# Two indirect transfers of an expert loop put behind relus by one-element VectorE copies

## The chip, the cores and the metric

The kernel runs on one core of a Trainium2 chip. The metric is the device time of one execution in microseconds, the median over several runs. Before the change it is 409.39 us (3 runs, 408.94 to 409.46).

## The reference

Attention with normalised queries and keys over 8 batches of 12 heads, 448 positions of width 64. Its output, read as 3584 tokens of width 768, goes through a mixture of 8 experts, each of which keeps at most 80 tokens:

```python
logits = x @ w_gate                       # x: attention output, 3584 x 768
expert_idx = np.argmax(logits, axis=1)    # gate_w: softmax share of that expert
out = np.zeros((N, D))
for e in range(E):                        # 8 experts
    tok_idx = np.where(expert_idx == e)[0]
    # over 80 tokens: keep the 80 with the largest gate_w
    h = np.maximum(x[tok_idx] @ w1[e], 0.0)
    out[tok_idx] = gate_w[tok_idx, None] * (h @ w2[e])
```

## The kernel before

Most of the time is the attention, which writes its unnormalised output rows (768 values and 12 row factors, so 780 floats) to the DRAM scratch `xr_dram`. The change lies wholly behind it, in the expert loop at the end. The text counts experts from 0 to 7, as the code does: the fourth is expert 3, the seventh is expert 6.

For each expert, `gather(e)` (L1107) issues an indirect DMA from the POOL queue that fetches 80 rows of 780 floats (250 KB) into a tile `xg`; `normal(e)` (L1153) multiplies them by their row factors in three VectorE instructions of 256 columns each (tile `xn`, L1157); `xpose(e)` (L1162) turns `xn` in six TensorE transposes (tile `pxt`, L1172) and copies the result to `xgT`. The loop (L1181) then does, for expert `e`, 48 matmuls with `w1` into `ph` (L1188) in two halves, each ended by a relu on ScalarE into `h_sb` (L1192); then `normal` and `xpose` of expert `e+1`; then the issue of `gather(e+4)`, which is held by a one-column memset of its tile (`wait=True`, L1118); then 16 matmuls with `w2` into two `py` (L1219); then two VectorE multiplications by the gate weights into `yo` (`weighted`, L1224); and `scatter` (L1203), an indirect DMA from the POOL queue that writes the 80 rows of `yo` to the output. Expert 0 differs: expert 1 is turned between its matmuls with `w2`, and `normal(2)` follows them. The last expert has four `py` of 192 columns and scatters in two halves.

Gathers 1, 2 and 3 are issued before the loop. POOL issues its transfers in the order of the program: gathers 1, 2, 3 and 4, scatter 0, gather 5, scatter 1, gather 6, and so on, each waiting at the head of POOL's queue until its own semaphores are there. They all travel in the DMA queue q0.

SP issues the weight loads, in queue q1, in program order: a part of expert 5's `w2` (`fetch_part`, L924; its last two of eight rows of blocks are held by a memset, L927, that stands inside `normal(1)`, behind its first multiplication), and, as each of experts 0 and 1 sets its weight buffers free, `w1` and `w2` of experts 6 and 7 (`fetch_late`, L242), 1536 KB each. The order of all this is the order of the program text: no scheduler moves it.

Of the kernel before, what the change touches and what calls it, by code (L numbers as in the profile page):

```python
# [15 lines left out]
U32 = mybir.dt.uint32  # L16
# [5 lines left out]
def kernel(  # L22
# [13 lines left out]
    nc = tc.nc  # L36

    B, H, S, D = q.shape
    N, DM = out.shape
    E = moe_w_gate.shape[1]  # L40
    F = moe_w1.shape[2]
    CAP = int(moe_capacity)
# [16 lines left out]
    FC = F // 128  # L59
# [139 lines left out]
    def load_weights(pool, e, slot, early=None):  # L199

        w1 = []
        for n, (c0, c1) in enumerate(((0, DC), ) if early is None else ((0, NE), (NE, DC))):
            if n == 0 and early is not None:
                w1.append(early)
                continue
            w1.append(pool.tile([128, c1 - c0, F], BF16, tag=f"w1_{slot}", name="w1_sb"))
        w2_sb = pool.tile([128, FC, DM], BF16, tag=f"w2_{slot}", name="w2_sb")
        w_tiles[e] = (w1, [w2_sb])

    def chunk(e, i, c):  # L210
        ts = w_tiles[e][i]
        return ts[0][:, c] if len(ts) == 1 or c < NE else ts[1][:, c - NE]
# [9 lines left out]
    def staged(e, i):  # L222
        return wb_dram[e - NW0, i].rearrange("(c p f) -> p c f", p=128, c=(DC, FC)[i])

    mark = cpool.tile([1, 4 * (E - NW0) + 2], BF16, name="mark")
# [12 lines left out]
    def fetch_late(e, parts=(0, 1)):  # L238
        for i in parts:
            ts = w_tiles[e][i]  # L240
            if len(ts) == 1:
                nc.sync.dma_start(out=ts[0][:], in_=staged(e, i))  # L242
            else:
                nc.sync.dma_start(out=ts[1][:], in_=staged(e, i)[:, NE:])
# [21 lines left out]
    with av_stack:  # L266
# [548 lines left out]
        for g in range(NG):  # L815
# [18 lines left out]
            if g < NG - 2:  # L834
                i = g % NQ
# [46 lines left out]
        for e in range(E):  # L882
            for i in range(2):
                n = 2 * e + i
# [35 lines left out]
    mpool = mlate[0]  # L920

    FE = FC - 2

    def fetch_part(c, held=False):  # L924
        t = w_tiles[NW0 + 2][1][0]
        if held:
            nc.vector.memset(t[:, c.start, 0:2], 0.0)  # L927
        nc.sync.dma_start(out=t[:, c], in_=staged(NW0 + 2, 1)[:, c])
# [80 lines left out]
    def rows_normal(i, xn, xg):  # L1009
        c = slice(256 * i, 256 * i + 256)  # L1010
        return (xn[:, c].rearrange("p (hh u d) -> p u hh d", hh=2, u=2),
                xg[:, c].rearrange("p (u hh d) -> p u hh d", hh=2, u=2),
                xg[:, DM + 4 * i:DM + 4 * i + 4].rearrange("p (u hh) -> p u hh", hh=2)
                .unsqueeze(3).to_broadcast([CAP, 2, 2, D]))

    for h in range(4):
        u, hh = divmod(h, 2)
        o = hh * 128 + u * D
# [85 lines left out]
            chosen(1, False)  # L1104
    outs = dram_disjoint_views(out, E + 1)
    xgs = {}
    def gather(e, wait=False):  # L1107

        if e == 1:
            xgs[e] = tpool.tile([128, 1024], F32, tag="beat", name="xg")[:CAP, :XW]  # L1110
        elif e % 4 == 3:
            xgs[e] = prep.tile([128, NJ + 1, 256], F32, tag="xb", name="xg")[
                :CAP].rearrange("p j d -> p (j d)")[:, :XW]
        else:
            xgs[e] = upool.tile([128, 2, S], F32, tag="us", name="xg")[:CAP].rearrange(
                "p u s -> p (u s)")[:, :XW]
        if wait:
            nc.vector.memset(xgs[e][:, 0:1], 0.0)  # L1118
        nc.gpsimd.indirect_dma_start(
            out=xgs[e], out_offset=None, in_=xr_dram[:, :],  # L1120
            in_offset=bass.IndirectOffsetOnAxis(ap=idxG[:, e:e + 1], axis=0))

    gather(1)
    idxT = tpool.tile([CAP, E], U32, name="idxT")
    nc.vector.tensor_copy(idxT[:, :], psc[:CAP, 1, :E])
# [27 lines left out]
    def normal(e, behind=None):  # L1153
        xg = xgs[e]
        xn = mpool.tile([CAP, DM], BF16, tag="xn", name="xn")
        for i in range(NQ):
            nc.vector.tensor_mul(*rows_normal(i, xn, xg))  # L1157
            if behind and not i:
                behind()
        return xn  # L1160

    def xpose(e, xn):  # L1162
        xgT = mpool.tile([128, DC, CAP], BF16, tag="xgT", name="xgT")
        pxt = mps.tile([128, DC, CAP], BF16, tag="pxt", name="pxt", bufs=1)
        if e > 1:
            o = [pxt[:, c] for c in range(DC)]
        else:
            first = tpps.tile([128, 2, 1024], BF16, tag="tp", name="pxt")[:, 0, :DC // 2 * CAP]
            o = [first[:, c * CAP:c * CAP + CAP] for c in range(DC // 2)]
            o += [pxt[:, c] for c in range(DC // 2)]  # L1170
        for c in range(DC):
            nc.tensor.transpose(o[c], xn[:, c * 128:(c + 1) * 128], identb[:CAP, :CAP])  # L1172
        if e > 1:
            nc.vector.tensor_copy(xgT[:], pxt[:])
        else:
            by_two(xgT, [first, pxt[:, :DC // 2].rearrange("p c t -> p (c t)")])
        xts[e] = xgT

    for e in range(2, 4):
        gather(e)  # L1180
    for e in range(E):  # L1181
        h_sb = mpool.tile([128, FC, CAP], BF16, tag="hsb", name="h_sb")
        for fh in range(2):
            ph = mps.tile([128, FC // 2, CAP], F32, tag="ph", name="ph")
            for f4 in range(FC // 2):
                fc = fh * (FC // 2) + f4
                for c in range(DC):
                    nc.tensor.matmul(ph[:, f4, :],  # L1188
                                     chunk(e, 0, c)[:, fc * 128:(fc + 1) * 128],
                                     xts[e][:, c, :],  # L1190
                                     start=(c == 0), stop=(c == DC - 1))
            nc.scalar.activation(h_sb[:, fh * (FC // 2):(fh + 1) * (FC // 2), :],  # L1192
                                 ph[:], AF.Relu)
        if e + 1 < E and e != 1:
            xn = normal(e + 1, (lambda: fetch_part(slice(FE, FC), True)) if not e else None)
        if 0 < e < E - 1:
            xpose(e + 1, xn)
        if e < E - 4:
            gather(e + 4, wait=True)
        DN = DM // 2  # L1200
        yo = mpool.tile([CAP, DM], F32, tag="yo", name="yo", bufs=3)

        def scatter(half=None):  # L1203
            if half is None:
                o, at, y, n = outs[e], idxT[:, e:e + 1], yo[:, :], N
            else:
                o = outs[e + half].rearrange("n (h d) -> (n h) d", h=2)
                at, y, n = idxL[:, half:half + 1], yo[:, half * DN:half * DN + DN], 2 * N
            nc.gpsimd.indirect_dma_start(  # L1209
                out=o[:, :], out_offset=bass.IndirectOffsetOnAxis(ap=at, axis=0),  # L1210
                in_=y, in_offset=None, bounds_check=n - 1, oob_is_err=False)

        pw = DN if e + 1 < E else DN // 2
        pys = [mps.tile([CAP, pw], F32, tag=("py", "py", "pz", "pxt")[i], name="py",
                        bufs=2 if i < 2 else 1) for i in range(DM // pw)]

        def product(i, fcs):
            for fc in fcs:
                nc.tensor.matmul(pys[i][:, :], h_sb[:, fc, :],  # L1219
                                 chunk(e, 1, fc)[:, i * pw:i * pw + pw],  # L1220
                                 start=(fc == 0), stop=(fc == FC - 1))

        def weighted(i):
            nc.vector.tensor_scalar(yo[:, i * pw:i * pw + pw], pys[i][:, :], gwT[:, e:e + 1],  # L1224
                                    None, op0=ALU.mult)

        if e + 1 < E:
            for fh in range(2):
                for i in range(2):
                    if not e and fh and i:  # L1230
                        xpose(1, xn)
                    product(i, range(fh * (FC // 2), (fh + 1) * (FC // 2)))
            if not e:
                xn = normal(2)
            for i in range(2):
                weighted(i)
            scatter()
        else:
            for fh in range(2):
                for i in range(2):  # L1240
                    product(i, range(fh * (FC // 2), (fh + 1) * (FC // 2)))
                    if fh:
                        weighted(i)
            scatter(0)
            for i in range(2, 4):
                product(i, range(FC))
                weighted(i)
            scatter(1)
        if NW0 + 3 + e < E:
            load_weights(wpool, NW0 + 3 + e, e)  # L1250
            fetch_late(NW0 + 3 + e)
# [35 lines left out]
```

## Time and profile before

| | |
|---|---|
| median of 3 runs | 409.39 us |
| the profiled execution, device time | 408.7 us |
| its span, first to last instruction | 407.0 us |
| its TensorE clock, mean granted | 0.999 of full speed |
| TensorE (PE) busy | 395.7 us, 97% |
| VectorE (DVE) busy | 352.2 us, 87% |
| ScalarE (ACT) busy | 320.6 us, 79% |
| GpSimd (POOL) busy | 90.2 us, 22% |
| bytes moved by DMA packets | 100.92 MB |

The profile is of one execution, and its times count from the span's first instruction. 1.7 us of the device time lie outside the span. A row of the timeline gives the start, the time until the last instruction of the group ended, the engine, the line and operation, the tiles written and read, how many instructions were merged, and in brackets how long the engine had been idle and what ended that. A DMA instruction's own duration is its issue; its transfer's time, from issue to landing, stands in the DMA view, where median and value are the same if one transfer was issued in the stretch.

### The profile page before, as it was taken

The page shows a single profiled execution, that of the slowest core. Times are in us where ns is not written, and L with a number is a line of the kernel's source. Part 1 is how long each engine was busy: PE and PEld are TensorE (multiplying, and loading weights), DVE is VectorE, ACT ScalarE, POOL GpSimd, SP SyncE. Part 2 cuts the span into 40 slices and gives each one's busy share as a digit, 9 for nine tenths or more (in the row PEclk, how much of TensorE's full clock was granted, in tenths as well). Part 3 has the DMA queues.
Part 4 walks back from the last instruction along what each step waited for, and adds up shares of the span by engine and source line. Part 5 has one row for each costly group of instructions (what it writes and reads, how often), then busy time and mean ns, then how long its engine had stood idle before and what let it go on. Part 6 is the DMA issues. An engine that isn't in the chain of part 4 may idle for free.

```text
span 407.0 us, 12628 instructions
## 1 busy us (share of the span) xinstructions
PE 395.7 (97%) x5285; PEld 195.4 (48%) x5285; DVE 352.2 (87%) x658; ACT 320.6 (79%) x508; POOL 90.2 (22%) x150
## 2 busy tenths in 40 slices
PE   8999999999999999999999999999999999999994
PEld 7334444444444444444444444444443453458884
DVE  5899987998999999997999999979999968876552
ACT  6899979997989889988899799979897877572110
POOL 7200002501031012220251024020512020154322
PEclk9999999999999999999999999999999999999999
DMA  7459999999989999989999999999999759798991
GB/s 244 144 159 212 272 296 257 273 217 304 254 223 264 246 260 263 294 205 228 243 306 217 243 278 230 289 237 285 219 205 297 161 195 374 245 277 274 342 333 52
DMA packets 76105, 100.92 MB, mean 248 GB/s; under 512 B 8448, under 2 KB 65280, under 8 KB 76048
## 3 DMA queue, kind: packets, MB, share of 16 engines
q1 hardware_dynamic: 60176, 70.99, 54.7%
q0 software_dynamic: 15872, 29.13, 39.3%
q8 instruction: 41, 0.67, 0.6%
q14 instruction: 16, 0.13, 0.1%
HBM read 101.11 MB, written 39.89 MB: 346 GB/s over the span
## 4 chain that ended last, share of the span: by engine, by line
PE 73%; DVE 12%; ACT 8%; issue 5%; POOL 2%; POOLq 0%; DVEq 0%
PE ps L423 26%; PE po L440 25%; PE zl L475 5%; DVE sm L458 4%; PE tp L381 4%; PE xp L381 3%; DVE ms L314 2%; DVE qn L344 2%; PE py L1219 2%; PE wps L894 2%; ACT at L426 1%; PE ph L1188 1%; POOL out_dram L1209 1%; ACT qkT L412 1%; PE mp L666 1%
## 5 line engine op out<-in xcount | busy, mean ns | idle before, releaser
L426 ACT ACTIVATE at<-ps 128x896 f32<-128x896 f32 x168 | 146.5, 930 | 4.5 <-PE ps L423 3.9
L423 PE MATMUL ps<-qkT 64*64 64x448 f32 x1344 | 147.3, 548 | 2.5 <-ACT row L624 1.3
L440 PE MATMUL po<-at,vt 64*64 64x448 f32 x1344 | 142.5, 537 | 0.0
L458 DVE TENSOR_TENSOR sm<-sm,at 128x896 f32<-128x896 f32 x120 | 130.7, 1089 | 3.4 <-ACT at L426 0.5
L440 PEld LDWEIGHTS po<-at,vt 64*64 64x64 f32 x1344 | 50.1, 133 | 74.0 <-issue 63.9
L423 PEld LDWEIGHTS ps<-qkT 64*64 64x64 f32 x1344 | 43.8, 132 | 66.6 <-issue 26.2
L314 DVE TENSOR_REDUCE ms<-sq 128x14 f32<-128x896 f32 (+1 forms) x50 | 52.1, 1043 | 6.9 <-ACT sq L307 6.8
L344 DVE TENSOR_TENSOR qn<-qk,rs 128x896 f32<-128x896 f32 (+1 forms) x47 | 50.5, 1077 | 1.3
L307 ACT ACTIVATE sq<-qk 128x896 f32<-128x896 f32 (+1 forms) x48 | 44.7, 930 | 2.0 <-DMA qk<-in_q_dram 1.1
L229 POOL COPY mark<-mark 1x1 bf16<-1x1 bf16 x22 | 7.8, 354 | 138.0 <-DVE mark L228 138.0
L743 ACT COPY xb<-xp 128x1024 f32<-128x1024 f32 x24 | 24.3, 1011 | 8.4 <-PE xp L381 8.3
L381 PEld LDWEIGHTS tp<-ident,qn 64*128 64x128 f32 x672 | 23.5, 139 | 12.1 <-issue 6.0
L381 PE MATMUL tp<-ident,qn 64*128 64x64 f32 x672 | 27.2, 226 | 0.3 <-DVE qn L344 0.3
L1192 ACT ACTIVATE h_sb<-ph 128x320 bf16<-128x320 f32 x16 | 7.0, 438 | 25.7 <-PE ph L1188 25.7
L447 ACT COPY us<-po 128x896 f32<-128x896 f32 (+1 forms) x24 | 21.4, 894 | 6.5 <-PE po L440 6.4
L456 DVE TENSOR_TENSOR sm<-at 128x896 f32<-128x896 f32 x24 | 26.0, 1084 | 0.1
L412 ACT COPY qkT<-tp 128x896 f32<-128x896 f32 x24 | 22.0, 917 | 3.3 <-PE tp L381 3.1
L410 ACT ACTIVATE qkT<-tp,gqk 128x896 f32<-128x896 f32 x23 | 23.6, 1025 | 0.0
L1219 PE MATMUL py<-w_sb,h_sb 128*80 128x384 bf16 (+1 forms) x144 | 22.4, 309 | 0.0
L475 PE MATMUL zl<-us,wgs 64*32 64x448 f32 x192 | 20.3, 540 | 0.0
L1224 DVE TENSOR_SCALAR yo<-py,gwT 80x384 f32<-80x384 f32 (+1 forms) x18 | 10.0, 568 | 11.7 <-PE py L1219 11.6
L475 PE MATMUL zl<-sm,zsel 64*32 64x448 f32 x192 | 20.1, 541 | 0.0
(202 smaller groups left out, 433.2 us busy)
## 6 DMA issues: line engine op xcount, KB each, us to landing
wb_scratch<-in_moe_w_dram POOLq DMA_DIRECT2D x20, 768.0 KB, 10.5
w_sb<-wb_scratch SPq DMA_DIRECT2D x8, 1536.0 KB, 11.4
vt<-in_v_dram SPq DMA_DIRECT2D x24, 448.0 KB, 7.6
out_dram<-zeros SPq DMA_DIRECT2D x28, 384.0 KB, 10.0
qk<-in_q_dram SPq DMA_DIRECT2D x23, 448.0 KB, 6.5
qk<-in_k_dram SPq DMA_DIRECT2D x23, 448.0 KB, 5.3
w_sb<-in_moe_w_dram POOLq DMA_DIRECT2D x6, 1536.0 KB, 14.9
xr_scratch<-xb SPq DMA_DIRECT2D x48, 192.0 KB, 6.7
```

Of the source, the lines that this page charges most:

```text
L307: nc.scalar.activation(o, x, AF.Square)
L314: nc.vector.reduce_sum(out=st[g]["ms"][:, a, lo:hi], in_=st[g]["sq%d" % a][:, lo:hi], axis=AX.X)
L344: e.tensor_mul(qn[:].rearrange("p (x hh) d -> p hh x d", hh=2)[:, h0:h1], qk[:, lo:hi].rearrange("p (hh x) d -> p hh x d", x=NX), rs[:, lo ...
L381: nc.tensor.transpose(o, w, one[p, p], tile_position=(p.start, 0))
L412: nc.scalar.copy(T[:], tp[:, :, :S])
L423: nc.tensor.matmul(ps[u * 64:u * 64 + 64, hh, :S], T1[d, u, x * 64:(x + 1) * 64], T0[d, u, :], start=True, stop=True)
L426: nc.scalar.activation(at[:], ps[:, :, :S], AF.Exp)
L440: nc.tensor.matmul(po[u][hh * D:(hh + 1) * D, u, :S], vt[p, hh * NX + x, :], at[p, hh, :], start=(x == 0), stop=(x == RD - 1))
L456: nc.vector.tensor_add(s["sm"][:], s["at0"][:], s["at1"][:])
L458: nc.vector.tensor_add(s["sm"][:], s["sm"][:], s["at%d" % x][:])
L475: nc.tensor.matmul(t[32 * c:32 * c + 32, r, :S], w, x, start=(i == 0), stop=(i == NQ - 1))
L1219: nc.tensor.matmul(pys[i][:, :], h_sb[:, fc, :], chunk(e, 1, fc)[:, i * pw:i * pw + pw], start=(fc == 0), stop=(fc == FC - 1))
```

## The change

`gather` gets an argument `behind`: where it is given, VectorE copies that one element into the gather's own tile first, so that the gather has to follow the copy, and the copy what wrote the element. Gather 3 leaves the place ahead of the loop and is called from inside `normal(1)`, behind its second multiplication, with an element that expert 0's second relu writes. Scatter 6 is kept back until the last expert's relus are programmed: VectorE copies one element of the last expert's second relu half to a scratch, then the 80 row numbers of expert 6 to a tile of their own, `at6`, and scatter 6 takes its rows from `at6`. Nothing else is moved.

```diff
-    def gather(e, wait=False):
+    def gather(e, behind=None, wait=False):
...
         if wait:
             nc.vector.memset(xgs[e][:, 0:1], 0.0)
+        if behind is not None:
+            nc.vector.tensor_copy(xgs[e][:1, 0:1], behind)
         nc.gpsimd.indirect_dma_start(
...
             nc.vector.tensor_mul(*rows_normal(i, xn, xg))
-            if behind and not i:
-                behind()
+            if behind:
+                behind(i)
...
-    for e in range(2, 4):
-        gather(e)
+    gather(2)
+
+    def second(i):
+        if i == 0:
+            fetch_part(slice(FE, FC), True)
+        elif i == 1:
+            gather(3, h_sb[:1, FC - 1, 0:1])
+
     for e in range(E):
...
-            xn = normal(e + 1, (lambda: fetch_part(slice(FE, FC), True)) if not e else None)
+            xn = normal(e + 1, None if e else second)
...
             for i in range(2):
                 weighted(i)
-            scatter()
+            if e + 2 < E:
+                scatter()
+            else:
+                last = scatter
         else:
+            nc.vector.tensor_copy(mark[:, :1], h_sb[:1, FC - 1, 0:1])
+            at6 = mpool.tile([CAP, 1], U32, name="at6", bufs=1)
+            nc.vector.tensor_copy(at6[:, :], idxT[:, e - 1:e])
+            last(at=at6)
             for fh in range(2):
```

How it stands on the engines, at the two places that matter. On VectorE, around `normal(1)` in expert 0's turn, before (`xn<-xg` are the multiplications, the memset of `w_sb` holds the weight part, the memset of `xg` holds gather 4; the names in brackets are semaphores, DMAHW those of transfers from SP's queue, DMASW those of POOL's):

```order
L1157 TENSOR_TENSOR xn<-xg 80x2x2x64 [waits DMASW5_49]
L927 MEMSET w_sb 128x1
L1157 TENSOR_TENSOR xn<-xg 80x2x2x64 x2
L1118 MEMSET xg 80x1
L1145 COPY xgT<-pxt 128x240 [waits DVE_49,PE_49]
```

and with the change (lines are those of the changed kernel):

```order
L1159 TENSOR_TENSOR xn<-xg 80x2x2x64 [waits DMASW5_49]
L927 MEMSET w_sb 128x1
L1159 TENSOR_TENSOR xn<-xg 80x2x2x64
L1120 CAST xg<-h_sb 1x1 [waits DMAHW5_49,DMAHW6_49,DMAHW4_49,DMAHW7_49,DMAHW2_49,Activation_49]
L1159 TENSOR_TENSOR xn<-xg 80x2x2x64
L1118 MEMSET xg 80x1
L1147 COPY xgT<-pxt 128x240 [waits DVE_49,PE_49]
```

The copy stands between the second and the third multiplication, ahead of gather 4's memset, and waits for five DMA semaphores beside ScalarE's. On VectorE in the last expert's turn, with the change (before, the two rows between the 384-column and the 192-column multiplications are not there):

```order
L1232 TENSOR_SCALAR yo<-py,gwT 80x384 [waits DMASW7_49,PE_49]
L1232 TENSOR_SCALAR yo<-py,gwT 80x384 [waits PE_49]
L1250 COPY mark<-h_sb 1x1 [waits Activation_49]
L1252 COPY at_6555<-idxT 80x1
L1232 TENSOR_SCALAR yo<-py,gwT 80x192 [waits DMASW0_49,DVE_49,PE_49]
L1232 TENSOR_SCALAR yo<-py,gwT 80x192 [waits PE_49] x3
```

The two copies stand between expert 6's last multiplication and the last expert's first. POOL's own order of transfers is the same before and after; what changes there is what gather 3 and scatter 6 wait for.

## Rows read from the trace of the kernel before

**Rows 1.** The page, busy time, share of the span, instructions of TensorE.

```profile
PE 395.7 (97%) x5285; PEld 195.4 (48%) x5285; DVE 352.2 (87%) x658; ACT 320.6 (79%) x508; POOL 90.2 (22%) x150
```

**Rows 2.** Windows of the expert loop and the end: length, busy, PEclk, DMA share, GB/s.

```profile
364.90:401.60 36.70, 36.58 (x570) 30.98 (x570) 19.61 (x51) 7.36 (x17) 12.80 (x14) 1.00 0.86 278
...
401.60:407.00 5.40, 0.00 (x0) 0.00 (x0) 0.36 (x1) 0.00 (x0) 1.14 (x2) 0.89 0.16 47
```

**Rows 3.** Timeline of TensorE: transposes of experts 1 and 3, matmuls between.

```profile
368.60 0.38 PE L1172 MATMUL pxt<-identb,xn 80*128 80x80 bf16 x6
...
374.01 1.88 PE L1188 MATMUL ph<-xgT,w_sb 128*128 128x80 bf16 x48
375.73 0.40 PE L1172 MATMUL pxt<-identb,xn 80*128 80x80 bf16 x6
```

**Rows 4.** Timeline of VectorE from 366.8 to 376.5.

```profile
366.88 0.77 DVE L1157 TENSOR_TENSOR xn<-xg 80x256 bf16<-80x256 f32 x2 [2.10 <-DMA xg<-xr_scratch,idxG]
...
367.93 0.06 DVE L1118 MEMSET xg<- 80x1 f32 x1
...
373.56 1.26 DVE L1224 TENSOR_SCALAR yo<-py,gwT 80x384 f32<-80x384 f32 x2 [1.47 <-PE py L1219]
374.75 1.08 DVE L1157 TENSOR_TENSOR xn<-xg 80x256 bf16<-80x256 f32 x3
```

**Rows 5.** Timeline of POOL from 364 to 376: gathers 3 and 4.

```profile
365.49 0.91 POOL L1119 DMA_INDIRECT xg<-xr_scratch,idxG  x1 [0.30 <-issue]
368.28 0.91 POOL L1119 DMA_INDIRECT xg<-xr_scratch,idxG  x1 [1.88 <-DVE xg L1118]
```

**Rows 6.** Timeline of ScalarE: the second relus of experts 0 and 7.

```profile
366.85 0.44 ACT L1192 ACTIVATE h_sb<-ph 128x320 bf16<-128x320 f32 x1 [0.42 <-PE ph L1188]
...
398.85 0.44 ACT L1192 ACTIVATE h_sb<-ph 128x320 bf16<-128x320 f32 x1 [0.36 <-PE ph L1188]
```

**Rows 7.** Timeline of VectorE: the memset that holds gather 7, behind DMA semaphores.

```profile
381.38 0.06 DVE L1118 MEMSET xg<- 80x1 f32 x1 [0.25 <-issue]
```

**Rows 8.** DMA issues, us to landing: gathers 3, 4 and 7, each window alone.

```profile
xg<-xr_scratch,idxG POOLq DMA_INDIRECT x1, 3.8
...
xg<-xr_scratch,idxG POOLq DMA_INDIRECT x1, 9.2
...
xg<-xr_scratch,idxG POOLq DMA_INDIRECT x1, 7.3
```

**Rows 9.** Timeline of SP's DMA queue: the held part, then three weight loads.

```profile
367.36 0.37 SPq L928 DMA_DIRECT2D w_sb<-wb_scratch  x1
367.89 0.40 SPq L242 DMA_DIRECT2D w_sb<-wb_scratch  x1
```

**Rows 10.** DMA from 369.0 to 372.6: packets; queue, packets, MB, share of 16 engines.

```profile
DMA packets 630, 1.14 MB, mean 315 GB/s; under 512 B 16, under 2 KB 254, under 8 KB 630
...
q1 hardware_dynamic: 630, 1.14, 95.6%
```

**Rows 11.** DMA from 372.6 to 377.6: the same.

```profile
DMA packets 751, 1.61 MB, mean 321 GB/s; under 512 B 35, under 2 KB 287, under 8 KB 750
...
q0 software_dynamic: 96, 0.41, 24.5%
```

**Rows 12.** Timeline of POOL from 393 to 404: scatter 6 and the last two.

```profile
398.02 0.91 POOL L1209 DMA_INDIRECT out_dram<-yo,idxT  x1 [3.71 <-DVE yo L1224]
400.92 0.91 POOL L1209 DMA_INDIRECT out_dram<-yo,idxL  x1 [1.99 <-DVE yo L1224]
402.91 0.92 POOL L1209 DMA_INDIRECT out_dram<-yo,idxL  x1 [1.08 <-DVE yo L1224]
```

**Rows 13.** Timeline of VectorE from 396 to 403: the last three groups of multiplications.

```profile
396.48 1.26 DVE L1224 TENSOR_SCALAR yo<-py,gwT 80x384 f32<-80x384 f32 x2 [1.54 <-PE py L1219]
399.90 0.74 DVE L1224 TENSOR_SCALAR yo<-py,gwT 80x192 f32<-80x192 f32 x2 [2.16 <-PE py L1219]
...
401.55 0.41 DVE L1224 TENSOR_SCALAR yo<-py,gwT 80x192 f32<-80x192 f32 x1 [0.25 <-PE py L1219]
```

More of the change, by code (lines that the diff above doesn't have):

```diff
@@ L1201, with scatter @@
         yo = mpool.tile([CAP, DM], F32, tag="yo", name="yo", bufs=3)
-        def scatter(half=None):
+        def scatter(half=None, at=None, e=e, yo=yo):
             if half is None:
-                o, at, y, n = outs[e], idxT[:, e:e + 1], yo[:, :], N
+                o, at, y, n = outs[e], idxT[:, e:e + 1] if at is None else at[:, :], yo[:, :], N
             else:
```

## The prediction

> **What bounds the kernel now.** I read the page first: TensorE is busy for 395.7 us of a span of 407.0 [rows 1]. The change touches only the expert loop, so I read the windows next. Between 364.90 and 401.60 TensorE is busy for 36.58 of 36.70 us at a granted clock of 1.00 [rows 2]: the loop has no gap in TensorE that an earlier or later transfer could give back. Behind it lie 5.40 us without a matmul [rows 2], in which the last multiplications, the last two scatters and their landing follow each other. So there are two questions: does a changed transfer become late enough to open a gap in TensorE, and does anything in the last 5.4 us move?
>
> The timelines answer where a gather is needed. Expert 3 is turned by TensorE at 375.73, directly behind 48 matmuls that began at 374.01 [rows 3]. Its rows are multiplied on VectorE from 374.75 on, as soon as the two multiplications of expert 1, begun at 373.56, are over [rows 4]; the three take 1.08 us, up to 375.83, and the transposes follow on their heels. There is no slack here: gather 3 has to land by 374.75, and each microsecond later is a microsecond of TensorE. Today it is issued at 365.49 [rows 5] and needs 3.8 us [rows 8], so it lands at 369.3, 5.4 us early.
>
> **Gather 3, step by step.** The copy stands behind the second multiplication of expert 1, which ends at 366.88 + 0.77 = 367.65 [rows 4]. The relu that it names ends at 366.85 + 0.44 = 367.29 [rows 6], before that: the wait for the relu itself costs nothing, it is the place in VectorE's order that counts. The copy also waits for five DMA semaphores, of stores long landed. The nearest row is the memset that holds gather 7, which has a like list of them ahead of it and stood 0.25 us in issue [rows 7]. That puts the copy at 367.9. Its duration no row shows: a one-column memset takes 0.06 us [rows 4], a 256-column multiplication 0.41 (half of 0.77, with the overlap); one element is nearest the memset, and I take 0.08. POOL starts a transfer 0.29 us after such a memset (367.99 to 368.28) [rows 4, 5]. Gather 3 is then issued at 367.98 + 0.29 = 368.27, 2.8 us later than today, and at the very moment at which gather 4 is issued today (368.28) [rows 5].
>
> On VectorE the insertion pushes the third multiplication to 368.0 to 368.4. TensorE turns expert 1 from 368.60 on [rows 3], so that is covered, with 0.2 us left; without that cover it would cost at most the 0.35 us of the insertion.
>
> What lies around 368.27 decides the landing. SP issues the held weight part at 367.36 and the first 1536 KB load at 367.89 [rows 9], both ahead of it. From below, the landing is gather 3's of today, 3.8 us with no weight load beside it [rows 8]: 372.1, and no loss. From above it is gather 4's, issued at this moment with the same loads ahead: 9.2 us [rows 8], landing at 377.5, a loss of 2.7 us. The nearest row is plainly gather 4's. The DMA view says why it took so long: from 369.0 to 372.6 the engines moved 630 packets, all of them of SP's queue [rows 10], although gather 4 had been issued at 368.28; only from 372.6 on does POOL's queue get a share, 24.5% [rows 11]. I take a little off the 9.2: today's gather 3, 250 KB, is still travelling until 369.3 and holds the weight loads back, and would no longer do so. At 315 GB/s [rows 10] that is up to 0.8 us; I take 0.6. So 8.6 us, landing at 376.9.
>
> Here a rule speaks for a shorter wait. The Trainium skill, "DMA: Bandwidth & Descriptors", section "Queues, rings and completion order", says that a DMA engine goes round its queues packet by packet, typically some 9 to 17 descriptors of one queue before the next. An estimate by it, at 17 descriptors of the 1.8 KB and the 20 GB/s per engine that the view gives, is a wait of 1.6 us and a landing at 373.7, in time. The trace does not agree: 630 packets of 16 engines are 39 on each without one of POOL's queue in between [rows 10], so the sum stays with the measured landing.
>
> VectorE's multiplications of expert 3 then start at 376.9 instead of 374.75, and TensorE's transposes slip by the same 2.1 us. What is queued behind the waiting VectorE instruction: the copy of `xgT`, gather 6's memset, expert 2's multiplications. They all belong to the turn that slips and are needed no earlier in it. On POOL, gather 4 follows gather 3 at 368.27 + 0.91 + 0.30 = 369.5, 1.2 us later than today, behind it in the same queue; it is needed 4.6 us (one expert) after gather 3, and one gather's bytes took less than that today [rows 8, 11]: covered. Later gathers are issued by memsets as now and have gained 2.1 us. None of the slip is made up, because TensorE is full up to the end [rows 2].
>
> **Scatter 6.** The last second relu ends at 398.85 + 0.44 = 399.29 [rows 6]. VectorE is idle there (from 397.74 to 399.90) [rows 13], so here the wait binds. Two small copies of 0.06 to 0.15 us each end at 399.5, well before the next multiplication. POOL issues at 399.8 instead of 398.02 [rows 12], and is free again 0.91 us later, at 400.7. The next scatter, 400.92 today, wants 0.30 after that: 401.0, or 401.3 if the issue takes 1.2 us. The last one comes at 402.91 [rows 12], and POOL is free for it at 402.5 at the latest. Its row holds a riddle: its input is ready at 401.55 + 0.41 = 401.96 [rows 13], and it starts 0.95 us later, where scatter 6 started 0.28 after its own (397.74 to 398.02) [rows 12, 13]. If that is tied to the scatter before it, the end moves by +0.1 to +0.4; if scatter 6's presence there caused it, by up to -0.67. I take 0.
>
> **The sum.** Against the profiled execution: 408.7 + 2.1 + 0.0 = 410.8. The median of the runs lies 0.7 above that execution, so 409.4 + 2.1 = **411.5 us**. Bounds of the main term are 0 and 2.7 us.
>
> **Rivals.** First, the gather gets its turn at once. If POOL's queue has the 24.5% of the engines from the start that it has later [rows 11], that is 79 GB/s and 3.2 us for 250 KB; added to 3.8 as a whole, landing comes between 372.1 and 375.3, and the loss is 0 to 0.5 us: 409.4 to 409.9, not slower by what can be measured. It decides at 374.75. For it speaks that gather 3 would be issued first in an empty POOL queue, where gather 4 had gather 3 ahead; against it, that gather 3's packets were gone by 369.3 and the 3.3 us after that were SP's alone.
>
> Second, that, and the last scatter loses its odd 0.67 us because scatter 6 is no longer between: 409.4 - 0.7 = 408.7, perhaps less. For it speaks only the riddle; against it, that scatter 6 comes nearer to the last two, not further away.
>
> Third, the gap in TensorE costs more than itself. Behind the last matmul the granted clock averages 0.89 over 5.4 us [rows 2], so the clock does fall when TensorE rests. If a gap of 2 us brought it to the lower of its levels (1.2 instead of 2.4 GHz) for one expert's turn, that turn of 4.6 us would double: 411.5 + 4.6 = 416. Against it, the window's mean of 0.89 says that the fall came late in those 5.4 us.
>
> That the change does nothing is no rival for gather 3: the copy is on VectorE's path whether the relu is late or not.
>
> **How the numbers follow.** Late gather, 411.5: 0.72, by itself 410.2 to 412.6 (landings of 7.4 us, near gather 7's 7.3, to 9.8, a little over the worst). In time, 409.4 to 409.9: 0.15. In time and the end shorter: 0.08. More than 412.8, by the clock or a still later landing: 0.05. The range reaches from 409.2 to 412.8 and leaves out the faster case and the slowest. A measurement of this kernel can tell about 0.2% from no change, 0.8 us, so 408.6 to 410.2 counts as the same: faster 0.06, same 0.19, slower 0.75.
>
> **What would show it.** Right: gather 3's issue near 368.3 and a landing of 8 to 9.2 us; VectorE idle before expert 3's multiplications, ended by that transfer; one gap of about 2 us in TensorE ahead of expert 3's transposes and none elsewhere; the same distances from there to the end. Wrong: gather 3 landing before 374.75, packets of POOL's queue between 369.5 and 372.6, or no gap in TensorE.

## The result and the profile after

| | before | with the change |
|---|---|---|
| median, us | 409.16 (8 runs, 408.39 to 409.76) | 412.93 (8 runs, 409.88 to 414.23) |
| ratio, 95% interval | | 1.0081 [1.0055, 1.0107] |
| profiled execution, device time, us | 408.7 | 413.63 |
| its span, us | 407.0 | 411.9 |
| its mean granted clock | 0.999 | 0.994 |

The change makes the kernel 0.8% slower, with an interval that leaves out 1. The ratio here and below is reckoned from the executions, not from the two medians, whose quotient is 1.0092 here. The executions fall into two groups: five of the eight have a mean granted clock of 0.994 and a median of 413.54 us, the other three 0.996 to 0.999 and a median of 411.34 us. This split is half of what follows.

The page of the changed kernel, TensorE's row first, answers to [rows 1]:

```profile
PE 398.6 (97%) x5285; PEld 196.7 (48%) x5285; DVE 353.0 (86%) x661; ACT 320.4 (78%) x508; POOL 90.2 (22%) x150
```

With the same 5285 matmuls TensorE is busy 2.9 us longer. Of this 0.56 us lie ahead of the expert loop (359.65 us busy against 359.09); the rest is in the loop. Something made matmuls slower there: a wait by itself adds idle time and little busy time. TensorE's waits in the expert loop, from the view of waits:

```profile
engine line waited for: us in total, times, longest us
PE pxt L1174 <- DVE xn L1159: 1.4, 1, 1.4
PE ph L1196 <- DVE xgT L1147: 0.2, 1, 0.2
```

There is one new wait, ahead of a group of transposes; the other one is there before, too. The windows of the loop, which begins at 365.97 here, with columns as in [rows 2], show both parts of the loss:

```profile
365.95:378.00 12.05, 11.10 (x188) 9.37 (x188) 5.19 (x17) 2.98 (x7) 4.92 (x6) 1.00 0.77 229
378.00:379.40 1.40, 0.80 (x8) 0.49 (x9) 1.04 (x3) 0.00 (x0) 0.00 (x0) 1.00 1.05 365
379.40:382.85 3.45, 3.45 (x13) 2.00 (x12) 0.41 (x2) 0.00 (x0) 0.91 (x1) 0.51 1.04 329
382.85:402.80 19.95, 19.95 (x313) 16.67 (x312) 11.86 (x27) 3.50 (x8) 5.15 (x5) 1.00 0.81 275
402.80:406.30 3.50, 3.50 (x58) 3.32 (x54) 1.36 (x5) 0.87 (x2) 1.30 (x2) 1.00 0.09 25
```

In the first two stretches TensorE rests for a part; in the third it is busy all the time, but PEclk is 0.51: the lower of its two levels, 1.2 GHz. Before, the same part of the loop is at 1.00 throughout [rows 2]. The timeline of TensorE says which matmuls these are, and answers to [rows 3]:

```profile
370.64 1.88 PE L1196 MATMUL ph<-xgT,w_sb 128*128 128x80 bf16 x48
372.36 0.38 PE L1174 MATMUL pxt<-identb,xn 80*128 80x80 bf16 x6
372.58 2.77 PE L1227 MATMUL py<-w_sb,h_sb 128*80 128x384 bf16 x16
375.18 1.88 PE L1196 MATMUL ph<-xgT,w_sb 128*128 128x80 bf16 x48
378.42 0.92 PE L1174 MATMUL pxt<-identb,xn 80*128 80x80 bf16 x6 [1.36 <-DVE xn L1159]
379.17 4.45 PE L1227 MATMUL py<-w_sb,h_sb 128*80 128x384 bf16 x16
383.46 1.24 PE L1196 MATMUL ph<-xgT,w_sb 128*128 128x80 bf16 x30
```

The rows at 372.58 and 379.17 are alike, 16 matmuls with `w2` each, of experts 1 and 2: 2.77 us and 4.45. The six transposes of expert 3, 0.40 us before, are strung out over 0.92, because each pair follows its own multiplication. VectorE tells what they wait for, and answers to [rows 4]:

```profile
368.70 0.77 DVE L1159 TENSOR_TENSOR xn<-xg 80x256 bf16<-80x256 f32 x2 [2.88 <-DMA xg<-xr_scratch,idxG]
369.07 0.06 DVE L927 MEMSET w_sb<- 128x1 uint32 x1
369.38 0.13 DVE L1120 CAST xg<-h_sb 1x1 f32<-1x1 bf16 x1
...
374.73 1.26 DVE L1232 TENSOR_SCALAR yo<-py,gwT 80x384 f32<-80x384 f32 x2 [1.54 <-PE py L1227]
377.94 1.09 DVE L1159 TENSOR_TENSOR xn<-xg 80x256 bf16<-80x256 f32 x3 [1.95 <-DMA xg<-xr_scratch,idxG]
```

The last row is the forecast late gather: VectorE stood 1.95 us for gather 3's rows. Its issue on POOL, and next to it SP's queue, answer to [rows 5, 9]:

```profile
369.79 0.91 POOL L1121 DMA_INDIRECT xg<-xr_scratch,idxG  x1 [3.56 <-DVE xg L1120]
371.00 0.92 POOL L1121 DMA_INDIRECT xg<-xr_scratch,idxG  x1 [0.30 <-DVE xn L1159]
```

```profile
369.17 0.37 SPq L928 DMA_DIRECT2D w_sb<-wb_scratch  x1
369.70 7.86 SPq L242 DMA_DIRECT2D w_sb<-wb_scratch  x4
```

Gather 3 goes out 0.62 us behind the held weight part and 0.09 behind the first large load. The DMA views, of its issue and of the two stretches behind it, answer to [rows 8, 10, 11]:

```profile
xg<-xr_scratch,idxG POOLq DMA_INDIRECT x1, 8.1
...
q1 hardware_dynamic: 541, 0.94, 94.1%
...
q1 hardware_dynamic: 332, 0.68, 60.3%
q0 software_dynamic: 123, 0.50, 40.6%
```

The gather takes 8.1 us to landing. From 370.1 to 373.5 (second row) every packet is of SP's queue, and so it is up to 374.0; POOL's queue shares the engines only from 374.0 to 378.0 (third and fourth row). Not all of this silence is a wait for SP. Scatter 6 of the kernel before, issued at 398.02 when SP's loads are over, has its first packet at 399.5, 1.5 us later, and in loads_later, below, where no large load is near, gather 3's first packet comes 1.7 us behind its issue (369.24 to 370.95). Here it comes 4.2 us behind it.

For the sum two more rows of before are needed, from its timeline of TensorE, which follow the last of [rows 3]:

```profile
375.96 2.77 PE L1219 MATMUL py<-w_sb,h_sb 128*80 128x384 bf16 x16
378.57 0.63 PE L1188 MATMUL ph<-xgT,w_sb 128*128 128x80 bf16 x13
```

From the start of expert 2's `ph` to that of its `py` it was 1.95 us (374.01 to 375.96) and is 3.99 (375.18 to 379.17): 2.04 more. From there to expert 3's `ph` it was 2.61 (to 378.57) and is 4.29: 1.68 more, the clock. Expert 0's turn takes 0.13 more (364.93 to 369.47 before, 365.97 to 370.64 now). That is 3.85; from the loop's first matmul to the end of the span it is 45.93 instead of 42.07, 3.86 more. The other 1.04 us by which the spans differ lie ahead of the loop, outside the change's reach; with the same first part gather_only, below, begins its loop at 365.07.

The end, on VectorE and POOL, answers to [rows 12, 13]:

```profile
404.21 0.14 DVE L1250 COPY mark<-h_sb 1x1 bf16<-1x1 bf16 x1 [1.57 <-ACT h_sb L1200]
404.28 0.13 DVE L1252 COPY at<-idxT 80x1 uint32<-80x1 uint32 x1
404.69 0.91 POOL L1217 DMA_INDIRECT out_dram<-yo,at  x1 [5.48 <-DVE at L1252]
...
405.91 0.91 POOL L1217 DMA_INDIRECT out_dram<-yo,idxL  x1 [0.30 <-DVE yo L1232]
406.44 0.41 DVE L1232 TENSOR_SCALAR yo<-py,gwT 80x192 f32<-80x192 f32 x1 [0.25 <-PE py L1227]
407.80 0.92 POOL L1217 DMA_INDIRECT out_dram<-yo,idxL  x1 [0.98 <-DVE yo L1232]
```

Scatter 6 is late, and the scatter behind it follows with 0.30 us between; the last one still starts 0.95 us after its input (406.85), as before.

### The profile page after: what moved, and what is told of

It is laid out like the page before. It is cut to its first block, busy times and chain, and to the rows that moved or that the text cites. A ratio compares the mean times of both kernels' runs of the same rounds, so it can differ in the third digit from the quotient of the medians.

```text
span 411.9 us, 12631 instructions
## 1 busy us (share of the span) xinstructions
PE 398.6 (97%) x5285; PEld 196.7 (48%) x5285; DVE 353.0 (86%) x661; ACT 320.4 (78%) x508; POOL 90.2 (22%) x150
## 5 line engine op out<-in xcount | busy, mean ns | idle before, releaser
L1227 PE MATMUL py<-w_sb,h_sb 128*80 128x384 bf16 (+1 forms) x144 | 24.1, 323 | 0.0
```

The costliest lines, as they stand in the source:

```text
L1227: nc.tensor.matmul(pys[i][:, :], h_sb[:, fc, :], chunk(e, 1, fc)[:, i * pw:i * pw + pw], start=(fc == 0), stop=(fc == FC - 1))
```

## The experiments

Kernels of one group ran on one chip beside its own runs of the kernel before: 409.07 us (31 runs) for the first group, gather_only to filled; 410.67 (27) for the second, loads_later, gather_first, later and pool_after; 409.11 (29) for the third, the last three rows. "Low clock" counts the executions with a mean granted clock of 0.995 or less; the kernel before has 6 of 87.

| kernel | median, us | ratio, 95% interval | low clock |
|---|---|---|---|
| gather_only | 412.62 | 1.0061 [1.0035, 1.0087] | 6 of 10 |
| scatter_only | 408.90 | 1.0002 [0.9975, 1.0030] | 1 of 10 |
| early_copy | 409.38 | 1.0007 [0.9986, 1.0027] | 0 of 10 |
| filled | 411.19 | 1.0054 [1.0032, 1.0076] | 0 of 10 |
| loads_later | 411.16 | 1.0018 [1.0002, 1.0034] | 0 of 10 |
| gather_first | 409.86 | 0.9985 [0.9973, 0.9997] | 0 of 10 |
| later | 413.32 | 1.0074 [1.0054, 1.0095] | 1 of 4 |
| pool_after | 410.87 | 1.0007 [0.9991, 1.0022] | 1 of 11 |
| gather_first_again | 409.24 | 0.9996 [0.9983, 1.0009] | 0 of 12 |
| held_last | 409.28 | 1.0016 [0.9993, 1.0038] | 3 of 12 |
| change_gather_first | 409.03 | 1.0000 [0.9984, 1.0017] | 1 of 12 |

**Each part alone.** gather_only has the change's first part and none of the second, scatter_only the second and none of the first. Against the change:

```diff
gather_only:
-            if e + 2 < E:
-                scatter()
-            else:
-                last = scatter
+            scatter()
         else:
-            nc.vector.tensor_copy(mark[:, :1], h_sb[:1, FC - 1, 0:1])
-            at6 = mpool.tile([CAP, 1], U32, name="at6", bufs=1)
-            nc.vector.tensor_copy(at6[:, :], idxT[:, e - 1:e])
-            last(at=at6)
scatter_only:
-    gather(2)
+    for e in range(2, 4):
+        gather(e)
...
-        elif i == 1:
-            gather(3, h_sb[:1, FC - 1, 0:1])
```

> The change without its second part: scatter 6 is issued as before, gather 3 stays behind the copy. If the loss is gather 3's lateness, this is as slow as the whole change, 1.005 to 1.011 times the kernel before, with VectorE idle for about 2 us ahead of expert 3's multiplications and gather 3 landing 8 us after its issue. If the end of the kernel (scatter 6 close to the last two scatters) makes the loss, this is within 0.2% of the kernel before.

> The change without its first part: gather 3 is issued ahead of the loop as before, scatter 6 waits behind the two small copies. If the loss is gather 3's lateness: within 0.2% of the kernel before, the last scatter still starting about 0.9 us after its input and the next to last at most 0.4 us later than before. If the end makes the loss: 2 to 4 us slower.

The loss is the first part's: its ratio, 1.0061, lies inside the interval of the whole change, and the second part's is 1.0002. The timeline of TensorE in gather_only, and its windows around the gap:

```profile
378.07 0.97 PE L1174 MATMUL pxt<-identb,xn 80*128 80x80 bf16 x6 [1.95 <-DVE xn L1159]
378.84 4.42 PE L1227 MATMUL py<-w_sb,h_sb 128*80 128x384 bf16 x16
```

```profile
376.00:378.75 2.75, 0.62 (x9) 0.24 (x6) 1.09 (x3) 0.44 (x1) 0.27 (x1) 1.00 1.03 303
378.75:382.25 3.50, 3.50 (x13) 2.14 (x14) 0.41 (x2) 0.00 (x0) 0.90 (x1) 0.51 1.05 340
```

It is the same picture: a gap (1.95 us), then half the clock. Six of its ten executions have the low clock and a median of 412.91; the other four 411.21. In scatter_only POOL's last three issues begin at 399.90, 401.12 and 403.01, the loop at 365.10: relative to the loop's start the last is 0.07 us earlier than before (37.91 against 402.91 - 364.93 = 37.98). Nothing moves at the end.

**The copy without the delay.** early_copy, and all kernels from here to later, are gather_only with one thing exchanged. This one puts the same kind of copy ahead of gather 3, but of an element that is there early, and issues it ahead of the loop:

```diff
+    gather(3, idxT[:1, 0:1])
...
-        elif i == 1:
-            gather(3, h_sb[:1, FC - 1, 0:1])
```

> Gather 3 behind a one-element copy with the same DMA semaphores to wait for, but from an element that is ready ahead of the loop, with the copy ahead of expert 1's multiplications (scatter 6 as before). If lateness is what costs, gather 3 is issued some 1 us before SP's held part, lands about 4 us later, long before expert 3 needs it, and the time is within 0.2% of the kernel before. If the copy and its waits cost by themselves, or the order on POOL does, the time stays 2 us or more above it.

Gather 3 is issued at 365.71, lands after 3.7 us, and there is no gap. The copy as such costs nothing; the moment of the issue does.

**The clock apart from the wait.** filled adds six matmuls of 512 columns ahead of expert 3's transposes, into a PSUM tile that nobody reads:

```diff
+        if e == 2:
+            fill = tpps.tile([128, 2, 512], F32, tag="tp", name="fill")
+            for i in range(6):
+                nc.tensor.matmul(fill[:, 0, :], identb[:, :],
+                                 tri[:, :].unsqueeze(1).to_broadcast([128, 4, 128]),
+                                 start=True, stop=True)
```

> As gather_only, with six matmuls of 512 columns without use (about 1.3 us at full clock) put on TensorE ahead of expert 3's transposes, into the gap. If part of the loss is that the granted clock falls behind the gap, it no longer falls, expert 2's sixteen matmuls with w2 take 2.8 us again instead of 4.45, and the time is 1.5 to 2 us below gather_only's, about 2 us above the kernel before. If the gap alone is the loss, the time is that of gather_only or up to 1 us more.

VectorE waits for gather 3 as before (1.63 us, landing after 8.0), but TensorE is busy meanwhile. Its timeline, and the windows around the place:

```profile
375.60 1.46 PE L1207 MATMUL fill<-tri,identb 128*128 128x512 bf16 x6
376.90 0.82 PE L1174 MATMUL pxt<-identb,xn 80*128 80x80 bf16 x6
377.56 2.77 PE L1233 MATMUL py<-w_sb,h_sb 128*80 128x384 bf16 x16
```

```profile
375.50:377.50 2.00, 1.91 (x19) 0.93 (x16) 1.09 (x3) 0.44 (x1) 0.42 (x1) 1.00 1.03 262
377.50:380.20 2.70, 2.70 (x20) 1.95 (x21) 0.83 (x3) 0.00 (x0) 0.91 (x1) 1.00 1.13 346
```

The 16 matmuls behind take 2.77 us again at a clock of 1.00, and none of the ten executions has the low clock. The median comes down by 1.43 us against gather_only, to where gather_only's executions without the fall are (411.21). The two ratios' intervals overlap; it is the trace and the count of executions (0 and 6 of 10) that tell them apart.

**The order of the issues.** Three kernels ask whether gather 3 is late because SP's loads went out ahead of it. loads_later holds SP's large loads until expert 0's last multiplication:

```diff
+            if not e:
+                nc.vector.memset(w_tiles[NW0 + 3][0][0][:, 0, 0:2], 0.0)
```

> As gather_only, with a memset of the first weight load's tile (expert 6's w1) on VectorE behind expert 0's last multiplication, so that SP's four 1536 KB loads start about 3.5 us later, behind gather 3. If the weight loads ahead of it in the engines make gather 3 late, it now lands 4 to 5.5 us after its issue, there is no gap ahead of expert 3, and the time is 0 to 1 us above the kernel before (the last loads may come late for expert 7). If gather 3 is slow for a reason of its own (the copy, its place on POOL), it still takes 8 us and the time is that of gather_only or more.

Gather 3 is issued at 369.24, 0.62 us behind the held part (368.62) as with the change, but the large loads go out at 372.22 only. VectorE has no wait for it, as its row shows, and TensorE no gap ahead of expert 3: it is the large loads that keep it back, not the held part.

```profile
376.40 1.08 DVE L1159 TENSOR_TENSOR xn<-xg 80x256 bf16<-80x256 f32 x3
```

What was won is partly paid elsewhere. At the end expert 7's `w2` is awaited, whose load was held up (timeline of TensorE):

```profile
401.07 2.15 PE L1227 MATMUL py<-w_sb,h_sb 128*80 128x192 bf16 x24 [0.65 <-DMA w_sb<-wb_scratch]
```

Expert 1's turn also took 5.43 us (370.24 to 375.67) instead of 4.54 (369.47 to 374.01 before); why is not shown.

gather_first keeps the loads nearly where they are and exchanges two neighbours inside `normal(1)`: gather 3's copy behind the first multiplication, the memset that holds SP behind the third.

```diff
         if i == 0:
-            fetch_part(slice(FE, FC), True)
-        elif i == 1:
             gather(3, h_sb[:1, FC - 1, 0:1])
+        elif i == 2:
+            fetch_part(slice(FE, FC), True)
```

> As gather_only, with the two tenants of expert 1's multiplications exchanged: gather 3's copy behind the first, the memset that lets SP go on behind the last. Gather 3 is issued near 367.9, SP's held part at 368.2 and the first load at 368.7. If what was issued first goes first, the gather lands 4 to 5 us after its issue and the time is that of the kernel before within 0.3%. If SP's packets get ahead all the same, since a POOL transfer's first packet comes later behind its issue than one of SP's, it takes 7 to 9 us and the time is that of gather_only.

The loss is gone. But gather 3 is not first on the DMA engines: it is issued at 367.99 and SP's held part 0.45 us behind it (368.44), yet up to 370.9 all packets are of SP's queue. What is different from the change: here POOL's packets come as the held part's last ones go, and share the engines with the first large load from its start; with the change the large load had them alone from 372.0 to 374.0.

Since the ratio lay a little below 1, the kernel was run again as gather_first_again; beside it ran held_last, the kernel before with the memset's move alone, and change_gather_first, the whole change with the exchange just shown. held_last, against before:

```diff
-            if behind and not i:
+            if behind and i == 2:
                 behind()
```

> The kernel with gather 3's copy behind the first multiplication of expert 1 and the held weight part behind the third, once more, because its ratio of 0.9985 [0.9973, 0.9997] lay below 1 by less than a measurement of this kernel can tell. If the order of the issues (gather 3 some 0.5 us ahead of the held part and 1 us ahead of the first 1536 KB load) is worth something by itself: ratio 0.997 to 0.999, interval below 1. If it only undoes the loss: ratio 0.999 to 1.001. Either way no gap in TensorE ahead of expert 3's transposes, and no execution with a mean granted clock of 0.995 or less beyond the few that the kernel before has (3 of 31 and 1 of 27 so far).

> Gather 3 stays ahead of the loop as in the kernel before; only the memset that holds SP's weight part moves from behind the first to behind the third multiplication of expert 1, so that SP's loads start some 0.7 us later. If the small gain of the kernel with gather 3 issued first came from the loads' later start: ratio 0.997 to 0.999, like that kernel. If it came from gather 3's place, or was none: ratio 0.999 to 1.001. Gather 4 should land earlier than the 9.2 us of the kernel before if its packets now get in ahead of the first big load's, and in 8 to 9.2 us if not.

> The whole change, both parts, with one thing exchanged inside normal(1): gather 3's copy stands behind the first multiplication and the memset that holds SP's weight part behind the third. If the loss comes from gather 3 being issued behind SP's loads and from nothing else in the change: ratio 0.998 to 1.001, no VectorE wait for a DMA ahead of expert 3's multiplications, granted clock at 0.996 or more in nearly all executions. If a wait on the relu as such, or the scatter part, costs something that the parts alone did not show: ratio 1.003 or more.

The small gain did not come back (0.9996 with 1 inside its interval), and held_last gains nothing either, so no version here is shown to be faster than the kernel before. In held_last gather 4 lands after 7.9 us instead of 9.2, which nobody waits for. Its first packet still comes 4.1 us behind its issue (369.27 to 373.4), after SP's. The later loads have a small price where they show: in the profiled execution of gather_first_again TensorE waits 0.69 us for expert 7's `w2`. change_gather_first is the decisive one: it is the whole change, both waits included, but for that exchange, and its ratio is 1.0000. From the loop's first matmul to the end of the span it is 42.09 us (367.11 to 409.2), against 42.07 before. Its timelines of POOL and SP:

```profile
369.91 1.19 POOL L1121 DMA_INDIRECT xg<-xr_scratch,idxG  x1 [2.54 <-DVE xg L1120]
```

```profile
370.36 0.37 SPq L928 DMA_DIRECT2D w_sb<-wb_scratch  x1
370.89 8.54 SPq L242 DMA_DIRECT2D w_sb<-wb_scratch  x4
```

Its gather 3 is issued 0.45 us ahead of SP's held part and 0.98 ahead of the large load. Here, too, the held part's packets go first: from 369.9 to 372.5 there are 135 packets, all of SP's queue, and POOL's 64 follow between 372.5 and 374.1. The DMA view of its issue and VectorE's timeline:

```profile
xg<-xr_scratch,idxG POOLq DMA_INDIRECT x1, 4.9
```

```profile
376.93 1.08 DVE L1159 TENSOR_TENSOR xn<-xg 80x256 bf16<-80x256 f32 x3
```

4.9 us instead of 8.1, and no wait. That it was issued earlier against the loop (2.80 us behind its start at 367.11, 3.82 with the change) is not the reason: in gather_first_again it goes out 3.64 behind the loop's start (369.08 - 365.44), also 0.98 ahead of the large load, and lands after 6.1 us, in time. The profiled execution of change_gather_first has a low clock too (0.993), and shows that this number alone doesn't say where the fall was. This is a window of it far ahead of the loop:

```profile
11.30:14.70 3.40, 3.40 (x20) 1.14 (x22) 1.97 (x3) 1.49 (x4) 2.22 (x3) 0.50 0.43 147
```

So the few low clocks of the kernel before and of held_last need not be in the loop, and in change_gather_first nothing of the sort is there: its loop (367.10 to 403.80) runs at 1.00, with TensorE busy for 36.59 of 36.70 us.

**Still later.** later calls gather 3 behind `normal(2)`'s second multiplication, 2.7 us behind SP's first large load (367.95). Against gather_only:

```diff
-        elif i == 1:
-            gather(3, h_sb[:1, FC - 1, 0:1])
...
-                xn = normal(2)
+                hs = h_sb
+                xn = normal(2, lambda i: gather(3, hs[:1, FC - 1, 0:1]) if i == 1 else None)
```

> As gather_only, with the copy still later, behind the second multiplication of expert 2, and so behind gather 4 in POOL's order: issue near 370.5. If the loss is the landing past 374.75, gather 3 lands near 378.5 to 380, the gap ahead of expert 3 is 3.5 to 5 us, the granted clock falls in it, and the time is 5.5 to 8 us above the kernel before. If the place of the copy in expert 1's turn is what costs, it is no slower than gather_only.

Issued at 370.61, now behind gather 4 (368.33), it makes VectorE wait 2.43 us, up to 378.59, 7.98 us behind the issue. TensorE's gap is as long as in gather_only, but in the profiled execution the clock stays (timeline, then windows):

```profile
379.06 0.92 PE L1174 MATMUL pxt<-identb,xn 80*128 80x80 bf16 x6 [1.84 <-DVE xn L1159]
379.81 2.77 PE L1225 MATMUL py<-w_sb,h_sb 128*80 128x384 bf16 x16
```

```profile
377.00:379.80 2.80, 0.78 (x13) 0.38 (x10) 1.09 (x3) 0.44 (x1) 0.37 (x1) 1.00 1.09 373
379.80:382.50 2.70, 2.70 (x21) 1.95 (x22) 0.87 (x3) 0.00 (x0) 0.90 (x1) 1.00 1.01 326
```

A gap of 1.36 us was followed by half the clock in the one trace, a gap of 1.84 us was not in the other. The length of the gap alone doesn't decide. What does isn't shown here. The loss of 5.5 to 8 us that was expected did not come: the landing was as expected, but the gap is 1.84 us and not 3.5 to 5, and the median lies 2.65 us above the kernel before. By time alone this kernel can't be told from gather_only (1.0074 and 1.0061, with four executions here); it is VectorE's wait that ties the loss to the landing. This execution also lost 1.3 us in two waits of TensorE for ScalarE's `h_sb`, which gather_only's trace doesn't have. The longer one, 0.82 us, lies in expert 1's turn, ahead of the gap: that turn takes 1.01 us more (5.55 for 4.54), and with the landing fixed the gap is shorter by as much.

**The last scatter.** pool_after is the kernel before with a POOL memset behind the last scatter, to see whether that scatter is late because it is POOL's last instruction:

```diff
+            nc.gpsimd.memset(mark[:, :1], 0.0)
```

> The kernel before with one more POOL instruction, a memset of one element, behind the last scatter. There the last scatter starts 0.93 us behind its input and every other 0.27. If that is because it is the last instruction ahead of the branch at the end of POOL's program, it now starts at 0.27 and the time is 0.5 to 0.7 us lower, 0.9985 of the kernel before. If it lies in the scatter (its distance from the one before it), it stays at 0.93 and the time is the same.

The last scatter still stands 1.07 us idle ahead of its start, and the time is the same. That explanation falls; no other was tried.

## Why the prediction was right, and where it was off

**That the gather comes late: right, and by the mechanism named.** The issue behind SP's loads, a landing of 8 to 9.2 us, packets of SP's queue alone in between, VectorE idle until the transfer, one gap in TensorE ahead of expert 3's transposes and none elsewhere: each is in the trace. I took 8.6 us to landing, it was 8.1. I took the issue 3.34 us behind the loop's start (368.27 - 364.93), it was 3.82: gather 1, whose rows the multiplications ahead of the copy need, landed 0.78 us later in this execution (368.70 - 365.97 = 2.73 us behind the loop's start, 1.95 before), and the way from there to the issue was 0.30 shorter than I had it (1.09 us for 1.39). That the two errors, 0.5 us each, nearly cancel is luck: expert 3's multiplications start 11.97 us behind the loop's start instead of 9.82, a slip of 2.15 against the 2.1 of the sum.

**That it is the place in VectorE's order and not the relu: right.** change_gather_first waits for the same relu and loses nothing.

**The first rival, the turn at once: false for this order of issues.** The Trainium skill, "DMA: Bandwidth & Descriptors", section "Queues, rings and completion order", has an engine go round its queues after some 9 to 17 descriptors, with 64 as the ceiling. The 541 packets between 370.1 and 373.5 are again 34 on each of 16 engines without one of POOL's queue in between, more than the typical number if a packet of the view is one descriptor. My "the trace does not agree" was still too strong: I left out the ceiling, which neither 34 nor the 39 of before reaches, and counted the 1.5 to 1.7 us behind an issue in which POOL's queue has no packet without a large load either. From 371.5 (1.7 us behind the issue) to 374.0 there are 478 packets, 30 on each engine. What the traces do show is the landing, and by that the sum was rightly made. The point from which it decides was the landing against the end of expert 1's multiplications, as put. With gather 3 issued ahead of the loads it lands on the other side of that point, though its packets are not first even then.

**That the insertion on VectorE is covered: right, as far as shown.** From the first of the three multiplications to the end of the third VectorE took 1.15 us (368.70 to 369.85) instead of 1.10 (366.88 to 367.98). The copy itself ran 0.13 us, not 0.08, and had no 0.25 us ahead of it: in this trace the list of DMA semaphores cost nothing. Expert 0's turn took 0.13 us longer, but the insertion is not shown to be the reason: in filled, which has it too, the turn takes 4.53 us (364.81 to 369.34), as before (4.54). Here the third multiplication ended behind the start of expert 1's transposes (369.64), since gather 1 had landed later.

**Scatter 6 at 0: right**, and measured alone: ratio 1.0002. Its issue came 34.80 us behind the loop's start in scatter_only, 34.87 by the text.

**The clock: this step failed.** The prediction said: "Against it, the window's mean of 0.89 says that the fall came late in those 5.4 us", and hence a chance of 0.05 for everything above 412.8. That argument took the delay of one fall, behind the last matmul, as a rule for every gap. Five of eight executions with the change, and six of ten with its first part alone, have the low clock, and both traces taken of them show it right behind the gap; for the other nine the place is inferred, from filled, where TensorE has no gap there and none of ten is low. The price was wrong too, in the other direction: not a whole turn doubled (4.6 us) but 16 matmuls with 4.45 us for 2.77, 1.68 us. With it the sum is 408.7 + 2.04 + 0.13 + 1.68 = 412.6, and with 1.04 for the stretch ahead of the loop 413.6, as the profiled execution has it (413.63). Without it, the forecast of 411.5 is what the executions with the clock up show: 411.34 with the change (three, 409.88 to 411.89), 411.21 with gather_only (four). The median of all, 412.93, lies 0.13 above the end of the stated range; the ratio on the 409.39 from which I started gives 412.7, just inside it. With these counts the likeliest case would have been "late gather, and then the clock" with about half the chance, at 411.5 + 1.7 = 413.2, and the range would have had to reach to 414.

## What to carry to other kernels

Before a transfer is moved behind another event, look at what the other queues issue within a microsecond of it: 0.98 us ahead of a large load or 0.09 behind it made 4.9 us or 8.1 of the same gather. The issue is not the first packet: look in the DMA view when each queue's packets begin. Where TensorE has no slack, price a new gap as its length plus the matmuls behind it at half the clock, with a fair chance for each, and look at the granted clock of the executions, not of one. When a wait turns out dear, exchange it with its neighbour on the same engine before giving it up.

## What was unexpected of the hardware

- A TensorE gap of 1.36 us was followed by 3.45 us at a granted clock of 0.51; one of 1.84 us in another kernel by none. The mean granted clock of one kernel also differs from execution to execution (0.994 in five, 0.996 to 0.999 in three with the change), though only the profiled ones show where it fell.
- In the profiled executions gather 3 (250 KB) landed after 3.6 to 6.1 us where it was issued ahead of SP's large loads, even by 0.98 us, and after 8.0 to 8.7 us where it was issued 0.08 or 0.09 us behind the first of them (8.1 with the change, 8.7 in gather_only, 8.0 in filled). Distances between these two were not tried.
- An indirect transfer of POOL had its first packet 1.5 to 1.7 us behind its issue where no large load was near (scatter 6 of the kernel before, gather 3 of loads_later), a load of SP 1.0 us behind it (held part: 369.17 to 370.15 with the change, 368.62 to 369.6 in loads_later). In gather_first and change_gather_first SP's held part was issued 0.45 us behind gather 3, and its packets still went ahead.
- The last scatter starts 0.95 us after its input where others take 0.3. It does so whether scatter 6 stands closely ahead of it or not, and whether or not an instruction of POOL follows. This stays open.
